# The second expert unit of a routed feed-forward tail takes the first expert's next 128 tokens, and the split weights of the first unit serve it too

## The chip, the cores and the metric

One Trainium2 chip, one NeuronCore. The metric is device time in microseconds (us) of one execution; lower is better. The core has a matrix engine (TensorE, PE), three engines for elementwise work (VectorE DVE, ScalarE ACT, GpSimd POOL), a queue that issues most transfers (SyncE, SP), and 16 DMA engines. An engine runs its instructions in program order.

## The reference

Three layers in a row on 2 x 768 tokens of width 512, all in float32:

```
x = attention(q, k, v)            # 8 heads of 64, window of 128 keys and 4 sink keys
x = moe_attention(x)              # 4 experts, each a causal attention over its own q, k, v; top 2 of 4
for b, s:                         # routed feed-forward ("moe2"), 8 experts
    fresh_e = argmax(x[b, s] @ w_gate)
    e = fresh_e if s == 0 or local_gate[b, s] < 0.5 else prev_e     # else the expert of the token before
    h = max(x[b, s] @ w1[e], 0)                                     # 512 -> 1024
    out[b, s] = softmax(logits)[e] * (h @ w2[e])                    # 1024 -> 512
```

Each token of the last layer goes through one expert only, and which one is known only on the chip.

## The kernel before

**Staging.** Tokens come in 12 tiles of 128 (`T = 12`, six of each batch). The two attentions run tile by tile. As tiles are finished their rows of x go to DRAM (`x2d`) and their router logits to `LG`, and `route` works out the expert of each token (`OH`), its rank in its expert (`rk`) and the rank modulo 128 (`slot`). `LT[j]` is a matrix for tile j that turns a list of chosen tokens into row numbers by a product on PE.

**Units.** The feed-forward then runs in units of 128 tokens of one expert: gather the rows by an indirect transfer on POOL (`ga`, L1563), transpose them (`ux`, L1543), a first group of 24 products with w1 (`unit_first`), ReLU (`hs`, L1603), transpose (`hT`), and a second group of 24 products with w2 (`unit_second`), then scale and scatter (`unit_end`, L1638 and L1641). Products are three float32r products each (L315 to L317), since every operand is split into a high and a low part. Remainders of up to 32 tokens go as at most four "pieces" in one unit of mixed experts (`pieces`, L1741), whose weights come through the ring `qw`.

**Weights of a unit.** Eight loads of 512 KB (`ld`, into the eight buffers `raw`), each skipped on the chip by a condition if the unit has the expert of the unit before (L1492); then eight splits (`sp`): ACT writes the high part (L1507), DVE the low part (L1515), into one of 11 buffers of the ring `w`. Five of these are buffers of the attention that have become free; six come with the pool `ff` and the buffer `wo`, after the attention's pools are closed (L1667 to L1679). A buffer goes back when the products that read it have been issued.

**Unit 0.** `first_expert` takes the expert with the most tokens among the first 8 tiles and lists its first 128 tokens, long before the last tile is routed, so that the first products of unit 0 lie under the rest of the attention. Its last quarter of weights, (3,1), shares memory with the router's scratch rows and loads after the last routing (`ld`, dependence on `K["routed"]`).

**The lists of all other units.** After the last tile, DVE works through two chains of small operations (L1400 to L1424), PE inverts the result (`inv`, L1430), DVE writes the row lists `gix` and `six` (L1432 to L1437), then the list of the pieces (L1445), then the table of experts `euf` (L1451 to L1459), which POOL copies to `eui` (L1569). SP reads `eui` for the addresses of every later load.

**The order of the work.** `Order.run` is a planner: each piece of work has an engine, an estimated duration, dependences, buffers and a priority. At each step it emits, for one engine, the piece that can start first by its estimates, and among those the one with the lowest priority number; so the program order of every engine is fixed before the launch. It runs twice over: once over everything up to unit 0's first half (L1666), where unit 0's work is marked to fill gaps only, and once over units 1 to 11 (L1808); whatever belongs to the second run stands behind the whole first run in each engine's queue. While PE has nothing to do before unit 1, the planner puts dummy products into the gap (`spin`, L396). Unit 0's second half (`unit_second(0, (1,))`) and its split (3,1) belong to the second run, and the split's low part waits for the gather of unit 1 (L1516).

## Time and profile before

| | |
|---|---|
| median of 3 runs | 427.0 us (423.95 to 429.46) |
| profiled execution | 427.42 us, span of the core 425.6 us, mean granted clock 0.987 |
| PE / DVE / ACT / POOL busy | 403.8 / 336.2 / 326.6 / 173.6 us |
| moved by DMA | 59.03 MB |

The span runs from the first to the last instruction on the core; the profiled execution is 1.8 us longer than its span. A busy PE includes dummy products.

### The profile page before, as it was taken

To read this page: it belongs to the slowest core of one execution; us is meant where nothing else is said; L and a number is where in the kernel's file an instruction comes from. 1 tells how busy PE (TensorE), PEld (TensorE's weight loads), DVE (VectorE), ACT (ScalarE), POOL (GpSimd) and SP (SyncE) were. 2 spreads that over 40 slices of the span, in tenths; PEclk is the share of its full clock that TensorE was granted. 3 is DMA by queue.
4 is the path that set the end of the run, shared out by engine and by line. 5 is a ranking of instruction groups with operands and counts; after the bars stand their busy time and mean duration, and the time that the engine had idled before them with its cause. 6 is when DMAs were issued, how large, how long until landed. Compare 5 with 4: busy or idle time off the path is not lost.

```text
span 425.6 us, 10370 instructions
## 1 busy us (share of the span) xinstructions
PE 403.8 (95%) x3322; PEld 316.1 (74%) x3322; DVE 336.2 (79%) x959; ACT 326.6 (77%) x767; POOL 173.6 (41%) x270
## 2 busy tenths in 40 slices
PE   7899999999999997999999999999999699999994
PEld 3579979978779867979767677556566488888883
DVE  3999598697898789588799879476886779898690
ACT  5799799679999697765796438477695978989780
POOL 8289995198886358401642043111020401100101
PEclk9999999999999999999999999999999979999999
DMA  9997288645978445220910247786658971100011
GB/s 181 170 203 197 67 154 159 122 101 101 180 111 160 101 89 111 52 75 13 339 74 27 74 153 267 245 244 203 202 168 261 393 296 46 49 27 26 24 28 55
DMA packets 102046, 59.03 MB, mean 139 GB/s; under 512 B 84319, under 2 KB 85855, under 8 KB 101984
## 3 DMA queue, kind: packets, MB, share of 16 engines
q1 hardware_dynamic: 99824, 51.47, 48.7%
q0 software_dynamic: 2160, 6.82, 4.6%
q8 instruction: 28, 0.46, 0.5%
q14 instruction: 34, 0.28, 0.2%
HBM read 86.58 MB, written 6.55 MB: 219 GB/s over the span
## 4 chain that ended last, share of the span: by engine, by line
PE 49%; issue 24%; DVE 18%; POOL 4%; ACT 3%; SPq 1%; POOLq 0%; another core or an unknown queue 0%; DMA 0%; ACTq 0%; DVEq 0%
PE bank L315 8%; PE bank L317 8%; PE bank L316 8%; PE bank L685 6%; DVE P L699 4%; PE bank L809 3%; PE bank L1741 3%; PE bank L410 3%; DVE pT L816 2%; DVE PX L699 2%; POOL out_dram L1641 2%; PE bank L1140 1%; PE bank L1543 1%; PE bank L780 1%; PE bank L826 1%
## 5 line engine op out<-in xcount | busy, mean ns | idle before, releaser
L1515 DVE TENSOR_TENSOR w<-raw,w 128x1024 fp32r<-128x1024 f32 x44 | 52.9, 1221 | 13.8 <-ACT w L1507 13.6
L709 ACT ACTIVATE P<-P,nm 128x260 f32<-128x260 f32 (+3 forms) x100 | 53.1, 535 | 10.9 <-DVE nm L699 10.6
L1507 ACT ACTIVATE w<-raw 128x1024 fp32r<-128x1024 f32 x44 | 45.8, 1062 | 9.6 <-DMA raw<-in_moe_w_dram 8.3
L769 POOL TENSOR_TENSOR raw<-PX,raw 128x512 f16<-128x512 f32 (+2 forms) x34 | 35.5, 1050 | 15.8 <-ACT raw L764 13.9
L1641 POOL DMA_INDIRECT out_dram<-yof,six x12 | 13.0, 1085 | 67.4 <-ACT yof L1638 66.2
L816 DVE TENSOR_TENSOR pT<-bank,pT 128x512 f16<-128x512 f32 (+1 forms) x50 | 30.7, 631 | 9.4 <-ACT pT L812 9.3
L1563 POOL DMA_INDIRECT xgf<-x2d,gix x9 | 10.4, 1152 | 66.3 <-PE bank L1543 60.8
L685 PE MATMUL bank<-kT,qT 64*128 64x260 f32 (+1 forms) x192 | 31.5, 398 | 2.1 <-POOL kT L583 1.1
L709 ACT ACTIVATE PX<-PX,nm 128x260 f32<-128x260 f32 (+4 forms) x60 | 30.5, 510 | 1.4 <-DVE nm L699 1.3
L315 PE MATMUL bank<-xT,wqk_h 128*128 128x256 f32 x96 | 29.5, 307 | 0.0
L410 PE MATMUL bank<-ident,raw 128*128 128x128 f32 x168 | 28.0, 289 | 0.5 <-DVE raw L949 0.3
L812 ACT ACTIVATE pT<-bank 128x512 f16<-128x512 f32 (+1 forms) x50 | 26.1, 550 | 2.8 <-PE bank L809 2.5
L809 PE MATMUL bank<-ident,P 128*128 128x128 f32 x180 | 26.8, 277 | 1.0 <-ACT P L709 0.7
L317 PE MATMUL bank<-xT,wqk_l 128*128 128x256 f32 x96 | 27.8, 289 | 0.0
L316 PE MATMUL bank<-xT,wqk_h 128*128 128x256 f32 x96 | 27.7, 288 | 0.0
L699 DVE CUSTOM_DVE_ANT_0 P<-bank,mask 128x260 f32<-128x260 f32 (+1 forms) x60 | 22.3, 399 | 5.4 <-POOL mask L332 4.7
L685 PEld LDWEIGHTS bank<-kT,qT 64*128 64x128 f32 x192 | 19.2, 185 | 9.2 <-issue 2.3
L1603 ACT ACTIVATE hs<-bank 128x512 f32<-128x512 f32 x24 | 14.3, 596 | 15.3 <-PE bank L317 15.3
L646 POOL TENSOR_SCALAR raw<-raw,s_sv 128x256 f32<-128x256 f32 x20 | 18.4, 930 | 18.0 <-ACT qT L416 9.1
L410 PEld LDWEIGHTS bank<-ident,raw 128*128 128x128 f32 x168 | 20.1, 162 | 7.0 <-DVE nm L699 2.0
L685 PE MATMUL bank<-k,q 64*128 64x256 f32 (+3 forms) x128 | 24.4, 466 | 0.1
L1515 DVE TENSOR_TENSOR xT<-raw,xT 128x1024 fp32r<-128x1024 f32 x16 | 19.2, 1217 | 6.6 <-ACT xT L1507 6.4
(456 smaller groups left out, 1476.8 us busy)
## 6 DMA issues: line engine op xcount, KB each, us to landing
raw<-in_moe_w_dram SPq DMA_DIRECT2D x104, 512.0 KB
qw<-in_moe_w_dram SPq DMA_DIRECT2D x64, 256.0 KB
raw<-in_v_dram SPq DMA_DIRECT2D x12, 256.0 KB
x2d<-x SPq DMA_DIRECT2D x12, 256.0 KB
raw<-in_q_dram SPq DMA_DIRECT2D x11, 256.0 KB
raw<-in_k_dram SPq DMA_DIRECT2D x11, 256.0 KB
pT<-raw SPq DMA_TRANSPOSE x46
raw<-in_moe_wv_dram SPq DMA_DIRECT2D x1, 512.0 KB
```

The lines of the kernel that those rows point to most:

```text
L315: nc.tensor.matmul(o, l[0], r[0], start=start, stop=False)
L316: nc.tensor.matmul(o, l[0], r[1], start=False, stop=False)
L317: nc.tensor.matmul(o, l[1], r[0], start=False, stop=stop)
L410: nc.tensor.transpose(p[:, j * 128:(j + 1) * 128], src(j), ident)
L685: nc.tensor.matmul(o, l, r, start=True, stop=True)
L699: nc.vector.tensor_tensor_reduce(p, s, sg["mask"], 0.0 if dead and st == 1 else -scale, gr["nm"] if si else 3.0e38, op0=OP.add, op1=OP.min ...
L709: nc.scalar.activation(p, p, AF.Exp, bias=gr["nm"], scale=-1.0, accum_out=sg["sum"]())
L769: nc.gpsimd.tensor_sub(shaped(pl[:, s_], dims), p_, shaped(ph[:, s_], dims))
L809: nc.tensor.transpose(R[tk][:, j * 128:(j + 1) * 128], R[gr["P"]][:, c:c + 128], ident)
L816: nc.vector.tensor_sub(pl[:, :n * 128], R[tk][:, :n * 128], ph[:, :n * 128])
L1507: nc.scalar.activation(R["w", u, c, hf][0], R["raw", u, c, hf], AF.Copy)
L1515: eng.tensor_sub(wl[:, :, s_], R["raw", u, c, hf][:, :, s_], f32(wh)[:, :, s_])
```

## The change

The first expert is given at least two units. Unit 1 is always the expert's tokens of rank 128 to 255. Their list needs only `rk`, `slot` and the first expert (`second_list`), so it is made directly behind the last tile's ranks, and the long chains that list all other units move, unchanged but for one operation, into a new function `lists`, in the planner's second run. `chosen` prepares one operation for each tile as it is routed. Unit 1 has no loads and no splits of its own: it reads unit 0's eight buffers of `w`, which unit 0 no longer gives back. Unit 2's loads compare with the expert of unit 0. Unit 0's second group of products and its split (3,1) go into the first run, without the wait for the gather. Buffers of the first attention move to a pool that is closed early (`fa`), and three of the ring's 11 buffers `w` now come from there, free before the attention ends; the ring keeps 11. The diff, cut:

```
-NW = 5
+NW = 2
+NWO = 3
...
     for t in range(n):
+        K["slot", j0 + t] = d_              # (in route; K["OH", j] likewise)
...
+            (0.08, lambda: V.tensor_scalar(fl0, oh0, float(C + PSZ + 1), None, op0=OP.mult))), [K["gix0"]], prio + 5)
+
+    def chosen(j, prio):
+        return add("DVE", 0.15, lambda: V.tensor_tensor_reduce(t80, OH[:, j, :], oh0, 1.0, 0.0, op0=OP.mult, op1=OP.add,
+                                                               accum_out=sl1[:, j:j + 1]), deps=[K["OH", j], K["first"]], prio=prio)
+
+    def second_list(prio):
+        cs = [chosen(j, at2(j // NT, j % NT, E1) + RPO + 3 if j < T - 1 else prio) for j in range(T)]
+        a = add("DVE", 0.1, lambda: V.scalar_tensor_tensor(u1f, rk, -float(C), slot, op0=OP.add, op1=OP.is_equal),
+                deps=[K["slot", j] for j in range(T)], prio=prio)
+        a = add("DVE", 0.1, lambda: V.tensor_tensor(u1_, u1f, sl1, op=OP.mult), deps=cs + [a], prio=prio)
+        def inv1():
+            for j in range(T):
+                nc.tensor.matmul(R["r_in1"][:, :1], LT[:, j, :], u1_[:, j:j + 1], start=j == 0, stop=j == T - 1)
+        c_ = add("PE", 0.4, inv1, deps=[a] + [K["LT", j] for j in range(T)], acq=[("B", "r_in1")], prio=prio)
+        K["gix1"] = add("DVE", 0.08, lambda: V.tensor_scalar(gix1, R["r_in1"][:, :1], -1.0, 0.0, op0=OP.add, op1=OP.max), ...
...
-    a = chain("DVE", ( ... L1400 to L1412 ... )), [K["cum", T], K["first"]], END)
-    ... L1414 to L1459 ...
+    second_list(END)
...
-                nc.sync.dma_start(raw, src, cond=R["e", u] != R["e", u - 1])
+                nc.sync.dma_start(raw, src, cond=R["e", u] != R["e", u - 1 if u > 2 else 0])
...
-        after = [K["ga", 1]] if u == 0 and (c, hf) == (3, 1) else []
+        after = []
...
+                              ("w", NWO, [([128, 2, 512], FR)] * 2)):      # in turnover
...
-        g0 = K["ga", u] = fo.add("POOL", 1.4, ga, deps=[K["gix"]] + ... + [K.get("eui")] * (u > 1) if u else ...
+        g0 = K["ga", u] = fo.add("POOL", 1.4, ga, deps=[K["gix"], K["eui"]] + ... if u > 1 else [K["gix1"]] + [K["out", j] for j in range(T)] if u else ...
-        for c in range(4 if u else 0):
+        for c in range(4 if u > 1 else 0):
             for hf in range(2):
                 ld(u, c, hf)
-        for c in range(2 if u else 0):
+        for c in range(2 if u > 1 else 0):
             for hf in range(2):
                 sp(u, c, hf)
...
-                        wh, wl = R["w", u, n, d // 2]
+                        wh, wl = R["w", 0 if u == 1 else u, n, d // 2]
-                rel = [("w", u, n, hf)] if (d0 + step) % 2 == 0 else []
+                rel = [("w", 0 if u == 1 else u, n, hf)] if u and (d0 + step) % 2 == 0 else []
...
-            for hf in range(2 if u or c == 2 else 1):
+            for hf in range(2 if u != 1 else 0):
                 sp(u, c, hf, bp + 5 * c + hf + BSP if u else bp + 5 * c + hf - 48)
...
-    unit_second(0, (0,))
+    unit_second(0)
...
+    def lists():
+        LP = -45
+        a = chain("DVE", (
+            (0.08, lambda: V.tensor_tensor(c8, cum[:, T, :], fl0, op=OP.max)),
+            ... L1400 to L1459 as before, the second chain behind K["gix1"] ...
+        K["eui"] = add("POOL", 0.1, lambda: P.tensor_copy(eui[:32 + PC], euf[:32 + PC]), deps=[K["euf"]], prio=LP)
+
     for u in range(TS):
         if u == 0:
             continue
+        if u == 1:
+            lists()
         unit_front(u)
         if u == 1:
-            sp(0, 3, 1, 10)
-            unit_second(0, (1,))
             probabilities()
```

## Rows read from the trace of the kernel before

**Rows 1.** The page, first line: the span of the core.
```profile
span 425.6 us, 10370 instructions
```

**Rows 2.** Windows: start:end, length, then busy time by engine, granted clock, DMA share, GB/s.
```profile
240.20:247.60 7.40, 6.97 (x53) 3.35 (x52) 6.47 (x39) 2.14 (x3) 1.84 (x4) 1.00 0.08 30
253.80:272.30 18.50, 17.89 (x114) 11.78 (x112) 16.74 (x29) 13.48 (x18) 4.47 (x4) 1.00 0.78 263
326.90:338.40 11.50, 8.49 (x43) 6.31 (x39) 7.59 (x8) 9.10 (x13) 2.90 (x3) 1.00 0.99 354
338.40:345.50 7.10, 6.43 (x16) 4.80 (x17) 5.82 (x6) 4.89 (x6) 1.57 (x1) 0.55 1.05 392
```

**Rows 3.** Windows of one line alone: L396 on PE, then L1515 on DVE.
```profile
240.20:247.60 7.40, 6.16 (x27) 2.40 (x27) 1.00 0.08 30
...
253.80:272.30 18.50, 11.81 (x10) 1.00 0.78 263
```

**Rows 4.** Timeline of PE, 240 to 254: start, length, line, out<-in, count.
```profile
240.20 0.82 PE L396 MATMUL bank<-v2h 128*128 128x512 f16 x3
241.05 0.66 PE L1543 MATMUL bank<-ident,hs 128*128 128x128 f32 x4
...
244.56 0.45 PE L1430 MATMUL bank<-v2h,v2h 128*128 128x23 f16 x12
...
247.59 0.58 PE L315 MATMUL bank<-xT,hT 128*128 128x512 f32 x1
...
253.79 0.40 PE L315 MATMUL bank<-w,uxf 128*128 128x512 f32 x1
```

**Rows 5.** Timeline of DVE, 235 to 249.
```profile
235.10 0.17 DVE L1273 CUSTOM_DVE_ANT_0 r_sc<-r_sc,r_fr 128x8 f32<-128x8 f32 x1
235.19 0.08 DVE L1273 DVE_READ_ACCUMULATOR2_ANT r_ms<- 128x1 f32 x1
...
239.09 0.36 DVE L1400 TENSOR_TENSOR v2h<-cum,k 128x192 f32<-128x192 f32 x1
...
239.75 0.14 DVE L1319 TENSOR_SCALAR slot<-rk 128x1 int32<-128x1 int32 x1
...
246.35 0.13 DVE L1459 TENSOR_SCALAR euf<-inc 1x1 f32<-1x1 f32 x1
...
247.01 1.28 DVE L1550 TENSOR_TENSOR hT<-bank,hT 128x512 fp32r<-128x512 f32 x2
248.21 1.22 DVE L1515 TENSOR_TENSOR wo_l<-raw,wo_h 128x1024 fp32r<-128x1024 f32 x1
```

**Rows 6.** Timeline of ACT, 241 to 249.
```profile
241.74 0.60 ACT L1546 ACTIVATE hT<-bank 128x512 fp32r<-128x512 f32 x1 [0.75 <-PE bank L1543]
242.23 1.05 ACT L1507 ACTIVATE wo_h<-raw 128x1024 fp32r<-128x1024 f32 x1
248.56 1.06 ACT L1507 ACTIVATE w<-raw 128x1024 fp32r<-128x1024 f32 x1 [5.28 <-DMA raw<-in_moe_w_dram]
```

**Rows 7.** Timelines of POOL and SP; last, issue to landing of the gathers into xgf.
```profile
246.07 1.05 POOL L1563 DMA_INDIRECT xgf<-x2d,gix  x1 [5.39 <-DVE dl L1456]
247.13 0.20 POOL L1569 CAST eui<-euf 36x3 int32<-36x3 f32 x1
...
248.38 0.10 SPq L1492 DMA_DIRECT2D raw<-in_moe_w_dram  x1
251.69 0.33 SPq L1729 DMA_DIRECT2D qw<-in_moe_w_dram  x1
...
321.33 23.01 SPq L1492 DMA_DIRECT2D raw<-in_moe_w_dram  x18
...
DMA to landing us min/median/max: 3.3/3.8/6.9
```

**Rows 8.** Timeline of PE and ACT at the first change of expert.
```profile
326.60 1.06 ACT L1507 ACTIVATE wo_h<-raw 128x1024 fp32r<-128x1024 f32 x1 [3.28 <-DMA raw<-in_moe_w_dram]
...
338.35 0.50 PE L315 MATMUL bank<-wo_h,ux 128*128 128x512 f32 x1 [1.83 <-ACT ux L1546]
```

More of the change, by code (lines that the diff above doesn't have):

```diff
@@ L292, in fused_kernel @@
     if banded and ns:
-        vbd = ring(work, 1, "vbd", ([96, H, D], F16))[0]
-        bufs["skp"] = ring(work, 2, "skp", ([128, 3, 32], F32))
+        vbd = ring(fa, 1, "vbd", ([96, H, D], F16))[0]
+        bufs["skp"] = ring(fa, 2, "skp", ([128, 3, 32], F32))
         for t in bufs["skp"]:
             nc.gpsimd.memset(t, 0.0)
-        bufs["skT"] = ring(work, 2, "skT", ([96, 128], F16))
+        bufs["skT"] = ring(fa, 2, "skT", ([96, 128], F16))
     R = {}
@@ L377, in fused_kernel @@
     wo_l = fw.tile([128, 2, XC], FR)
-    kT = work.tile([128, HP, (NT - 1) * BS + C], F32)
+    kT = fa.tile([128, HP, (NT - 1) * BS + C], F32)
     k2 = [work.tile([128, 2, S], F32, name=f"k2_{b}") for b in range(B)]
@@ L1215, in fused_kernel @@
     n0_ = rt.tile([128, 1], F32)
+    fl0 = rt.tile([128, E2], F32)
+    c8 = rt.tile([128, E2], F32)
+    sl1 = rt.tile([128, T], F32)
+    u1f = rt.tile([128, T], F32)
+    u1_ = rt.tile([128, T], F16)
+    gix1 = rt.tile([128, 1], I32)
     evv = rt.tile([128, E2], F32)
@@ L1299, in route @@
                  deps=[b_], rel=[rb], prio=prio)
+        for t in range(n):
+            K["OH", j0 + t] = b_
         def count():
@@ L1320, in route @@
                                            op0=OP.bitwise_and))), [t_ if n > 1 else c_, K.get(("cum", j0))], prio, rel=())
+        for t in range(n):
+            K["slot", j0 + t] = d_
         join([d_, t_], [cb], prio)
```

149 lines of the change are left out of this document (76 added, 73 removed).

## The prediction

> **What bounds the kernel now.** I read the span first [rows 1], then the timelines of all engines around the last tile's routing, then windows over the stretches after it. The sum is made against the profiled execution's 427.42 us (span 425.6, 1.8 outside it); it lies 0.4 above the median of the three runs, whose own spread is 5.5 us. About 2% is what a measurement of this kernel can tell from no change.
>
> PE sets the pace nearly everywhere from the last tile on, with two holes. The first is the one the change aims at. At 240.20 PE has finished unit 0's first products and goes to dummy products: 27 of them fill 6.16 of the next 7.40 us [rows 3]; real work there is one set of transposes and the inversion [rows 4]. Unit 0's second group starts at 247.59 and unit 1's first product at 253.79 [rows 4]. What PE waits for is DVE: from 239.09 to 246.48 it works through the list chains, and the low part of unit 0's transposed activations comes only behind them, at 247.01, the low part of split (3,1) at 248.21 [rows 5]. The high part had been ready since about 242.3 [rows 6].
>
> From 253.8 to 272.3 PE is busy 17.89 of 18.50 us [rows 2], with ten splits on DVE beneath it [rows 3]. So unit 1's splits are hidden work, and taking them out pays nothing directly. The second hole is at the first change of expert: from 326.9 to 338.4 PE works 8.49 of 11.5 us, with DMA busy 0.99 at 354 GB/s, then 16 products take 6.43 us at a granted clock of 0.55 [rows 2]. ACT stands there behind loads (3.28 us once) and unit 6's first product starts at 338.35 [rows 8].
>
> **The change part by part.**
>
> *Unit 1's list.* `slot` of the last tile is written at 239.75 [rows 5], done by 239.9. Behind it come two small DVE operations at 0.15 each with a hop, the inversion on PE (12 products, at most the 0.45 of the old one [rows 4]) and one DVE operation. With hops I put `gix1` at 241.4 and the gather at 241.5 instead of 246.07 [rows 7]. Landing 3.8 us later [rows 7] it is in at 245.3; the 6.9 of the slowest gather would make it 248.4, 1.2 later than I need it.
>
> *Unit 0's second group.* It follows the first group on PE directly. 24 products and unit 1's four transposes took 6.20 us (247.59 to 253.79) [rows 4]. With the transposes of `hs` (0.66 at most) and the inversion (0.45 at most), PE has 7.2 us of work, from 240.2 to about 247.4. Two inputs can be late. The first `hT` needs a low part on DVE (0.64 for one of the two [rows 5]): DVE is free of the long chains, so I allow 0.6 of waiting, between 0 and 1.5. Split (3,1) has its high part from 242.23 to 243.3 [rows 6] and would have its low part, 1.22 us [rows 5], at 244.6; it is wanted for the last six products, after 246, so it costs nothing. If its load came 2 us late it would cost 0.5.
>
> *Unit 1's start.* Its transposes belong to the second run and stand on PE behind all of unit 0. After them PE must wait for ACT (0.60 [rows 6]) and, after two products, for DVE (0.64); with hops that exposes 1.2 us, between 0.8 and 1.6. Unit 1's products then start in effect at 240.2 + 7.2 + 0.6 + 1.2 = 249.2 instead of 253.79: 4.6 earlier.
>
> *What comes back.* The lists' own inversion and the four-way `spread` that follows stay on PE, later: 0.6 in all. The PE waits of 0.61 in 253.8 to 272.3 [rows 2] came with the splits of unit 1 and go away. These cancel.
>
> *The twelve `chosen` operations.* Each is an operation with its read, 0.17 + 0.08 [rows 5]. Eight become ready together right after the first expert is known and four at one per tile; the whole is 3 us of DVE, which is not idle in that stretch. If all of it were on the path it would cost 3.0, if none, 0. Most tiles leave DVE gaps between dependent operations and the splits of unit 0 can move, so I take 0.3.
>
> *The moved chains.* They start behind split (3,1) on DVE, 244.6, and take the 7.4 us of before [rows 5] plus one evicted low part: end 252.7, `eui` on POOL at 252.9 (it was 247.33 [rows 7]). Queued behind it are SP's loads and unit 2's splits: ACT's first split came 1.2 us after `eui` [rows 6, 7], so now at 254.1, its low part done at 256.4. Unit 2's products are wanted one unit after 249.2, that is 24 + 24 products and three sets of transposes, 2 x 6.20 [rows 4]: at 261.6. The margin is 5.2 us, so this costs nothing as forecast. For the eight splits together: they are wanted by about 272, and the same 18.5 us of DVE held ten splits before [rows 3]; eight fit in 15. The ring is no limit: three buffers are free at once, unit 1 gives back the others as it goes.
>
> *Loads skipped.* Unit 1's loads took 0.10 us of SP each [rows 7] because they were skipped; unit 1 already had unit 0's expert. Dropping them saves no bytes, and the extra unit that the change could force on a smaller first expert does not arise.
>
> Sum: 4.6 gained, 0.3 lost, the rest cancels: 4.3 from 427.4, **423.1 us**. With the waits at their low ends (1.0 less), no cost of `chosen` (0.3) and the PE items, which I took at their full lengths, 0.8 shorter, it is 421; with the waits at their high ends (1.3 more) and 1.4 instead of 0.3 for `chosen` it is 425.5. All of `chosen` on the path would make it 427.1.
>
> **The rivals.**
>
> *The gain is lost again at the change of expert.* The first piece load was issued at 251.69, 4.4 after `eui` [rows 7]; now it would be 257.3, 5.6 later, while PE is 4.6 ahead. The loads of unit 6 stand behind all piece loads in SP's program order (first one at 321.33 [rows 7]), and DMA runs full from 326.9 [rows 2]. If the piece loads keep their pace, unit 6's loads start no earlier and its first product stays at 338.35: the time is then 427.4, or up to 428 with the 0.3 of `chosen`. Against it: before 272 DMA is busy only 0.78 [rows 2], and the piece loads are paced by PE's consumption as much as by the chip.
>
> *The second hole shrinks too.* PE loses there 3.0 + 0.7 us of waiting, and 16 products at 0.40 each instead of at most 0.24 lose 2.5 [rows 2, 4]: 6.2 us. ACT and DVE have eight splits less to do on the way and the planner lays out every queue anew; if unit 6's weights come early enough, the time falls to 417; with half of it, 420. Against it: the splits of units 2 to 5, and the 8 MB of two experts, stay.
>
> *Slower: unit 2 waits for its weights.* If the moved chains are stretched, because the planner puts evictions and split parts between their operations, `eui` slips. Up to 258.1 it costs nothing (margin 5.2). Beyond that each microsecond is one of PE, and after about 4.6 more, at 262.7, the gain is gone. Such a stall has a second price: after the waits of the second hole the granted clock was 0.55, that is the lower level, 1.2 GHz, for most of it, and 16 products lost 2.5 us [rows 2]. `eui` at 263 with one such spell gives 427.4 + 0.6 (0.3 of it `chosen`) + 2.5 = 430.5. The chains would have to take over twice their 7.4 us; DVE was 90% busy from 253.8 to 272.3 [rows 2], so it is not excluded.
> The Trainium skill, page "TensorE: Matmul & The Clock Gate", section "What's actually happening", says that throttled is the default state and activity releases it. By that rule an idle stretch where there used to be dummy products speaks against the change; the trace agrees at the second hole, and by the rule alone a spell there would cost the same 2.5 us that the row gives.
>
> **How the numbers follow.** Forecast, 421 to 425.5: 0.50. Gain lost at the change of expert, 425.5 to 428: 0.22. Second hole shrinks, 416 to 421: 0.18. Slower, 428 to 437: 0.10. The predicted time is the forecast's, 423.1. For the range I leave out the upper rival and the lower third of the third case: 417.5 to 428.0 leaves out about 0.16. Faster by over 2% means below 418.5: half to two thirds of the third case, and a little for a tail of the forecast, 0.14 together. Slower by over 2%, above 435.5: 0.03. Within 2%: 0.83.
>
> **What would show it.** Right: the gather of unit 1 near 241.5; no dummy products between unit 0's two groups beyond one or two microseconds; unit 0's last product near 247 and unit 1's first near 249; the list chains on DVE from about 244.6, `eui` near 253; 8 splits fewer on ACT and on DVE; unit 6's first product near 334 at the change of expert. Wrong: `slot` of the last tile later than 240.5 (`chosen` or the new buffer order on the path); a PE wait for a split in unit 2; unit 6's first product still near 338; a gap before unit 1 that is longer than 2 us.

## The result and the profile after

The changed kernel takes 432.33 us (median of 20 runs, 427.35 to 436.83); the kernel before takes 425.69 us beside it (median of 20, 422.20 to 429.46). The ratio is 1.012, 95% interval 1.0084 to 1.0156: slower by about 5 us (clear of the noise, though under 2%), where 423.1 was forecast and 428.0 was the top of the range. Eight of the twenty executions, the profiled one (435.82 us) among them, lie over 1.5% above the fastest at a granted clock of 0.973 to 0.983, and the ratio leaves such executions out. A second profile of the same kernel was taken later (430.81 us); both are used.

The first line of the page after answers to [rows 1]:
```profile
span 434.1 us, 10311 instructions
```
The timeline of DVE after, from the first expert's list to the last list (start, length, line, out<-in); it answers to [rows 5]:
```profile
203.08 0.16 DVE L1370 TENSOR_SCALAR gix<-bank 128x1 int32<-128x1 f32 x1 [1.17 <-PE bank L1368]
...
203.43 0.16 DVE L1378 CUSTOM_DVE_ANT_0 t<-OH,oh 128x8 f32<-128x8 bf16 x1
...
204.99 0.08 DVE L1378 DVE_READ_ACCUMULATOR2_ANT sl<- 128x1 f32 x1
...
247.82 0.15 DVE L1329 TENSOR_SCALAR slot<-rk 128x1 int32<-128x1 int32 x1
...
249.53 0.16 DVE L1391 TENSOR_SCALAR gix<-bank 128x1 int32<-128x1 f32 x1 [0.19 <-PE bank L1389]
...
253.67 0.16 DVE L1772 TENSOR_TENSOR c<-cum,fl 128x8 f32<-128x8 f32 x1
...
262.18 0.08 DVE L1829 TENSOR_SCALAR euf<-inc 1x1 f32<-1x1 f32 x1
```
The last tile's `slot` is written at 247.82, not at 239.75; 1.5 us of this lie before the first expert's list. The list chains take 8.6 us behind it (253.67 to 262.26), where they took 7.4. Eight `chosen` operations stand at 203.43 to 205.07.

The timeline of PE after, between the last `slot` and unit 2; it answers to [rows 4]:
```profile
245.82 0.39 PE L398 MATMUL bank<-v2h 128*128 128x512 f16 x1
...
250.15 0.39 PE L317 MATMUL bank<-xT,hT 128*128 128x512 f32 x1
...
253.37 0.60 PE L398 MATMUL bank<-v2h 128*128 128x512 f16 x2
...
256.55 0.60 PE L1519 MATMUL bank<-ident,xgf 128*128 128x128 f32 x4
256.99 1.67 PE L398 MATMUL bank<-v2h 128*128 128x512 f16 x7
258.31 0.58 PE L317 MATMUL bank<-wqk_h,uxf 128*128 128x512 f32 x1
...
272.19 2.80 PE L1714 MATMUL bank<-qw,v2h 128*32 128x512 f32 x10
276.08 2.89 PE L1714 MATMUL bank<-qw,v2h 128*32 128x512 f32 x6 [1.09 <-DMA qw<-in_moe_w_dram]
278.90 0.50 PE L317 MATMUL bank<-wo,hT 128*128 128x512 f32 x1
```
The 27 dummy products [rows 3] are down to ten (1, 2 and 7), and unit 0's second group (250.15) follows its first directly: this part of the change does what it says. From `slot` to unit 1's first product it is 10.49 us instead of 14.04. Then 16 piece products take from 272.19 to 278.90; with their weights there, 16 took 1.92 us in the trace before:
```profile
277.09 1.92 PE L1741 MATMUL bank<-qw,v2h 128*32 128x512 f32 x16
```

POOL, SP and ACT after, a view each; they answer to [rows 6, 7]:
```profile
250.46 1.05 POOL L1539 DMA_INDIRECT xgf<-x2d,gix  x1 [1.71 <-DVE gix L1391]
262.33 0.18 POOL L1830 CAST eui<-euf 36x3 int32<-36x3 f32 x1 [10.82 <-DVE euf L1829]
```
```profile
266.89 6.09 SPq L1702 DMA_DIRECT2D qw<-in_moe_w_dram  x11
274.02 5.25 SPq L1464 DMA_DIRECT2D raw<-in_moe_w_dram  x7
```
```profile
274.12 1.06 ACT L1479 ACTIVATE wo_h<-raw 128x1024 fp32r<-128x1024 f32 x1 [2.62 <-DMA raw<-in_moe_w_dram]
```
`eui` stands 4.2 us behind unit 1's first product (262.51 against 258.31); before it stood 6.5 ahead of it. SP sends eleven piece loads from 4.4 us after `eui`, and only then unit 2's loads, which are skipped but have to be reached; so ACT's first split of unit 2 starts 11.6 us after `eui`.

Windows of the profile after (length, busy time by engine, granted clock, DMA share, GB/s); they answer to [rows 2]:
```profile
240.20:247.80 7.60, 7.60 (x30) 5.71 (x31) 3.23 (x15) 1.37 (x3) 0.00 (x0) 0.69 0.11 37
247.80:258.30 10.50, 10.50 (x63) 7.75 (x62) 7.17 (x29) 3.34 (x5) 1.73 (x2) 1.00 0.24 74
258.30:276.80 18.50, 16.19 (x107) 9.81 (x106) 10.35 (x43) 6.80 (x11) 6.02 (x7) 1.00 0.62 205
334.00:346.00 12.00, 10.65 (x53) 6.38 (x51) 6.60 (x7) 6.96 (x10) 1.28 (x1) 1.00 1.02 381
```
In the 18.5 us behind unit 1's first product PE is busy 16.19, where it was 17.89 before. At the first change of expert the granted clock stays at 1.00 (0.55 before), with DMA as full as it was. From unit 6's first product to unit 7's, in the trace before, in after_again and in e2 (below: the kernel before with the `chosen` operations alone, whose plan behind unit 1 is close to that before):
```profile
338.35:354.65 16.30, 15.63 (x61) 12.36 (x62) 13.45 (x14) 12.96 (x16) 3.62 (x3) 0.79 0.68 252
345.62:358.00 12.38, 12.38 (x62) 10.20 (x60) 11.32 (x12) 11.19 (x15) 2.00 (x2) 1.00 0.66 242
346.27:358.74 12.47, 12.47 (x61) 10.20 (x60) 11.31 (x12) 11.15 (x15) 2.00 (x2) 1.00 0.61 227
```
So the profiled execution before has 3.8 us there that e2 does not have, and they go with a low clock: 0.21 of 16.3 us, 3.4, is clock that is missing.

**Where the time went.** The table cuts each profiled execution in four, from the timelines: from the first expert's list (`gix`, 203.08 above) to the last `slot`; from there to unit 1's first product; from there to unit 7's first activation; and to the end. Up to `gix` every kernel has the same instructions in the same order (200.5 to 203.6 us, which is how much executions differ). Beside the first and the third of these stands the mean granted clock of the stretch. `eui` is its end against unit 1's first product.

| kernel | list to last slot | its clock | slot to unit 1 | eui against unit 1 | unit 1 to unit 7 | its clock | to the end | span |
|---|---|---|---|---|---|---|---|---|
| before | 38.1 | 1.00 | 14.0 | -6.5 | 103.9 | 0.97 | 68.0 | 425.6 |
| after | 44.7 | 0.89 | 10.5 | +4.2 | 107.7 | 1.00 | 68.1 | 434.1 |
| after_again | 39.6 | 1.00 | 10.5 | +4.2 | 107.5 | 1.00 | 68.1 | 429.1 |
| e2_before_chosen | 42.7 | 0.96 | 14.6 | -7.4 | 100.8 | 1.00 | 68.2 | 430.0 |
| e1_chosen4 | 40.5 | 0.96 | 10.3 | +4.2 | 107.4 | 0.98 | 68.1 | 428.3 |
| e13_due_end | 39.3 | 1.00 | 10.5 | +4.2 | 108.3 | 0.98 | 68.1 | 426.6 |
| e9_chosen_end | 39.2 | 0.96 | 10.5 | +4.2 | 105.6 | 1.00 | 68.1 | 424.1 |
| e12_eui_late | 38.2 | 1.00 | 10.5 | +10.5 | 111.7 | 0.97 | 68.1 | 431.3 |
| e4_qu3 | 43.8 | 0.88 | 10.5 | +4.2 | 111.0 | 0.97 | 68.2 | 434.9 |
| e7_behind | 40.6 | 0.96 | 10.3 | +4.2 | 109.5 | 0.98 | 68.1 | 429.5 |
| e6_regs | 40.5 | 0.96 | 10.3 | +4.2 | 104.8 | 1.00 | 68.1 | 426.8 |
| e11_end_regs | 38.2 | 1.00 | 10.5 | +4.2 | 104.4 | 1.00 | 68.2 | 423.7 |
| e10_all | 38.1 | 1.00 | 10.5 | +4.2 | 116.6 | 0.96 | 68.0 | 435.5 |
| e15_prob_late | 38.1 | 1.00 | 10.5 | +3.7 | 106.9 | 1.00 | 68.1 | 425.2 |
| e3_lists_early | 43.2 | 0.92 | 16.8 | -9.4 | 101.8 | 1.00 | 68.2 | 431.9 |
| e16_lists_fill | 40.1 | 0.96 | 12.5 | -2.1 | 105.9 | 0.98 | 68.1 | 428.1 |
| e17_lists_fill2 | 39.5 | 0.96 | 12.5 | -2.1 | 101.4 | 1.00 | 68.1 | 422.5 |
| e18_spread_late | 40.4 | 0.96 | 10.7 | -0.3 | 103.5 | 1.00 | 68.2 | 425.4 |
| e19_inv_late | 39.4 | 0.96 | 10.9 | -1.0 | 104.3 | 0.98 | 67.7 | 424.1 |

From before to after the span grows by 8.5: 1.5 before the first changed instruction, 6.6 up to the last `slot`, 3.5 back up to unit 1, 3.9 lost from there to unit 7, and nothing behind. Two of these numbers are not the price of the change at a like clock. The 6.6 fell at a clock of 0.89; at 1.00, in after_again, it is 1.5. And the 3.9 is too small, for the stretch before has the low clock behind unit 6's first product in it: from unit 1's first product to unit 6's it is 84.6 us before and 85.4 in e2, but 92.3 and 92.0 in the two profiles after. So some 7 us are lost there. The expected gain of 3.5 is there, and the two losses outweigh it.

### The profile page after: what moved, and what is told of

The parts are those of the page before. It is cut to its first block, busy times and chain, and to the rows that moved or that the text cites. A ratio compares the mean times of both kernels' runs of the same rounds, so it can differ in the third digit from the quotient of the medians.

```text
span 434.1 us, 10311 instructions
## 1 busy us (share of the span) xinstructions
PE 409.8 (94%) x3317; PEld 319.3 (74%) x3317; DVE 332.0 (76%) x980; ACT 320.1 (74%) x759; POOL 171.2 (39%) x270
## 4 chain that ended last, share of the span: by engine, by line
PE 42%; issue 26%; DVE 13%; DMA 6%; ACT 6%; POOL 4%; SPq 2%; POOLq 0%; another core or an unknown queue 0%; ACTq 0%; DVEq 0%
PE bank L317 7%; PE bank L687 6%; PE bank L319 6%; PE bank L318 6%; PE bank L412 3%; DMA qw<-in_moe_w_dram 3%; PE bank L811 3%; DVE PX L701 2%; DVE pT L818 2%; DMA xg<-x2d,gix 2%; DVE P L701 2%; POOL out_dram L1614 2%; DMA pT<-raw 1%; PE bank L1714 1%; PE bank L782 1%
## 5 line engine op out<-in xcount | busy, mean ns | idle before, releaser
L771 POOL TENSOR_TENSOR raw<-PX,raw 128x512 f16<-128x512 f32 (+2 forms) x34 | 35.5, 1051 | 16.3 <-ACT raw L766 16.0
L1487 DVE TENSOR_TENSOR wo<-raw,wo 128x1024 fp32r<-128x1024 f32 x28 | 33.6, 1221 | 7.2 <-ACT wo L1479 7.2
L1614 POOL DMA_INDIRECT out_dram<-yof,six x12 | 12.5, 1046 | 62.8 <-ACT yof L1611 61.3
L1479 ACT ACTIVATE wo<-raw 128x1024 fp32r<-128x1024 f32 x28 | 28.8, 1057 | 3.5 <-DMA raw<-in_moe_w_dram 2.4
L412 PEld LDWEIGHTS bank<-ident,raw 128*128 128x128 f32 x168 | 20.7, 164 | 6.9 <-DVE nm L701 1.7
L1539 POOL DMA_INDIRECT xgf<-x2d,gix x9 | 8.9, 985 | 40.5 <-PE bank L1519 37.7
L811 PEld LDWEIGHTS bank<-ident,P 128*128 128x128 f32 x180 | 20.3, 142 | 3.2 <-ACT P L711 1.0
```

Source lines behind the costliest of these rows:

```text
L412: nc.tensor.transpose(p[:, j * 128:(j + 1) * 128], src(j), ident)
L771: nc.gpsimd.tensor_sub(shaped(pl[:, s_], dims), p_, shaped(ph[:, s_], dims))
L811: nc.tensor.transpose(R[tk][:, j * 128:(j + 1) * 128], R[gr["P"]][:, c:c + 128], ident)
L1479: nc.scalar.activation(R["w", u, c, hf][0], R["raw", u, c, hf], AF.Copy)
L1487: eng.tensor_sub(wl[:, :, s_], R["raw", u, c, hf][:, :, s_], f32(wh)[:, :, s_])
```

## The experiments

Theory A: the `chosen` operations bring the last `slot` late. Theory B: the late list (`eui`) costs the stretch from unit 1 to unit 7. A rival to A is that unit 0's work, now spread among the last tile's, does it; a rival to B that the stretch is bound by something that the list does not touch. Edits are cut to the lines that matter. Some expectations count the stretch to unit 7 from unit 1's first activation, about 3.6 us behind its first product: 102.0 there is the table's 105.6.

### e1: eight `chosen` taken out

The sums for tiles 0 to 7 exist already, for the first expert's own list.
```
-            (0.1, lambda: V.reduce_sum(sl0, se0, axis=AX.X)),
+            (0.1, lambda: V.reduce_sum(sl1[:, :JE], se0, axis=AX.X)),
-        cs = [chosen(j, ...) for j in range(T)]
+        cs = [chosen(j, ...) for j in range(JE, T)]
```


> Theory A (the eight `chosen` instructions for tiles 0 to 7, which stand on VectorE at 203.4 to 205.1 us of the changed kernel, make the planner order the work of tiles 8 to 11 anew, and that is what brings the last tile's `slot` 6.6 us later): here `chosen` is issued for tiles 8 to 11 alone and the sums of tiles 0 to 7 are taken from the sums that the first expert's list already needs, so the order on VectorE up to tile 9 is again that of the kernel before. Then the last tile's `slot` falls back from 247.8 to about 240 to 242 us, unit 1's first product from 258.3 to 251 to 253, TensorE's granted clock between 230 and 250 us stays at 1.00, and the time is 5 to 7 us below the changed kernel: ratio to the kernel before 0.995 to 1.003. What then remains against 423 us is the late list (theory B: 4 us lost in the first pieces). Rival (unit 0's second group or the other split that now fill gaps in the first run, or the new places of the buffers, delay the last tile): `slot` stays at 246 us or later and the ratio at 1.010 to 1.015.

Measured: 430.47 us, ratio 1.014 (1.0092 to 1.0188). Theory A's ratio (0.995 to 1.003) did not come. In the profile the last `slot` comes 40.5 us behind the list and the span is 5.8 below that of after, but the runs show no gain (1.014 beside 1.012): the first profile of after has the low clock in it. `slot` is 2.4 us later than before, still, and the loss behind unit 1 is all there (107.4).

### e2: `chosen` alone, added to the kernel before

```
+    for j in range(T - 1):
+        chosen(j, at2(j // NT, j % NT, E1) + RPO + 3)
```


> The kernel before with nothing but the `chosen` instructions added (tiles 0 to 10, same place and same due times as in the changed kernel; their result is not used). Theory A: their busy time is 2.3 us, but the order of tiles 8 to 11 becomes that of the changed kernel, so the last tile's `slot` comes at 245 to 248 us instead of 239.8, unit 1's first product 5 to 8 us later, and the ratio to the kernel before is 1.012 to 1.018. Rival (fills or buffers are the cause): `slot` at 239.5 to 242, ratio 0.999 to 1.004.

Measured: 431.46 us, ratio 1.0149 (1.0100 to 1.0198): the kernel before becomes slower by as much as the whole change makes it, from operations whose result nobody uses. DVE's `slot` operations in this kernel, tiles 8 and 9, 10, 11:
```profile
232.83 0.15 DVE L1323 TENSOR_SCALAR slot<-rk 128x2 int32<-128x2 int32 x1
235.78 0.14 DVE L1323 TENSOR_SCALAR slot<-rk 128x1 int32<-128x1 int32 x1
246.36 0.14 DVE L1323 TENSOR_SCALAR slot<-rk 128x1 int32<-128x1 int32 x1
```
Before, tiles 8 and 9, then 10 (tile 11 is in [rows 5]):
```profile
222.35 0.16 DVE L1319 TENSOR_SCALAR slot<-rk 128x2 int32<-128x2 int32 x1
231.02 0.15 DVE L1319 TENSOR_SCALAR slot<-rk 128x1 int32<-128x1 int32 x1
```
Tiles 8 and 9 are routed 8.5 us later behind the list than before (29.2 against 20.7), and ACT's split of unit 0 that waits for that routing starts at 228.7 instead of 217.1. That is Theory A; unit 0's moved work is not in this kernel, so it is not needed for the delay. The clock of this stretch is 0.96, so the 4.6 us by which the last `slot` is later hold a part that is the clock's.

### e13: all `chosen` kept, only their due time changed

```
-        cs = [chosen(j, at2(j // NT, j % NT, E1) + RPO + 3 if j < T - 1 else prio) for j in range(T)]
+        cs = [chosen(j, prio) for j in range(T)]
```


> The changed kernel with one thing altered: the due time of the `chosen` instructions of tiles 0 to 10 is that of the end and not that of their tiles. All 12 are still issued, eight of them still at 203 to 206 us, so their busy time (2.5 us) is all there; but the order of the other instructions on VectorE is again that of the kernel before up to its row 731 (tile 10's routing). If the new order is what delays the last tile (theory A as the second round left it), `slot` falls back as in the run with the three late instructions: 38 to 40 us behind the first expert's list (`gix0`; before 38.2, changed 44.7), ratio 1.005 to 1.011. If the busy time of the instructions does it, `slot` stays 42 us or more behind `gix0` and the ratio 1.011 to 1.016.

Measured: 429.02 us, ratio 1.0093 (1.0062 to 1.0124). DVE's `slot` operations:
```profile
222.34 0.17 DVE L1329 TENSOR_SCALAR slot<-rk 128x2 int32<-128x2 int32 x1
231.03 0.15 DVE L1329 TENSOR_SCALAR slot<-rk 128x1 int32<-128x1 int32 x1
239.75 0.15 DVE L1329 TENSOR_SCALAR slot<-rk 128x1 int32<-128x1 int32 x1
```
All twelve operations are issued, eight of them still between 200.8 and 207.1, and the last `slot` is back at 39.3 us behind the list, at a clock of 1.00. Of their busy time 1.2 us reaches the path (39.3 against 38.1 before, and against 38.1 and 38.2 in e10, e11, e12 and e15, which have this order without the eight). What the change has beyond that comes with their due time: given that of their tiles, the planner lets them go ahead, and lays out the work of tiles 8 to 11 behind them in another order. The second profile of the change, below, shows how that order costs time. In the runs the gain over the change (1.0141 there) is small, and the intervals overlap.

### e9: e1 with the other three due at the end

```
-    chosen(j, at2(j // NT, j % NT, E1) + RPO + 3 if j < T - 1 else prio)
+    chosen(j, prio)
```


> The first experiment's kernel, with the `chosen` instructions of tiles 8 to 10 given the due time of the end instead of that of their tiles; the order on VectorE is then that of the kernel before up to its row 731 (tile 10's routing). Theory A, carried on: of the 2.8 us by which the last tile's `slot` was still late in the first experiment (242.6 against 239.8 us) the three instructions between tiles 8 to 10 make 1 to 2.5, and `slot` comes at 239.8 to 241.5, unit 1's first product at 250.5 to 252, ratio 1.004 to 1.012 (the loss in the pieces stays). Rival (the rest is unit 0's earlier work among the last tile's, or one execution's difference from another): `slot` at 242 or later and the ratio as in the first experiment, 1.010 to 1.017.

Measured: 427.72 us, ratio 1.0079 (1.0042 to 1.0116), `slot` at 239.9 and unit 1's first product at 250.4, both as expected to 0.1 us. Beside after_again (1.0141), e13 and e9 take a third or a little more of the loss away. What stays is put down to Theory B, which e12 tests.

### after_again: a second profile of the change

> The changed kernel once more, unaltered, for a second profile beside the others on one chip. Theory A: `slot` 43 to 45 us behind `gix0`, theory B: 103 to 105 us from unit 1's to unit 7's first activation, and the two rounds of first pieces in 5.5 to 7 us; ratio 1.010 to 1.016. If the first profile was only a disturbed execution, `slot` stands 38 to 40 us behind `gix0` here.

Measured: 431.13 us, ratio 1.0141 (1.0084 to 1.0198). B's numbers repeat to 0.3 us (107.5 after 107.7), though e1, e9 and e13, which have the same order of instructions from unit 1 to unit 7, spread from 105.6 to 108.3. A's do not repeat: `slot` is 39.6 us behind the list here, 44.7 in the first profile, from one program. The expectation had named 38 to 40 as the sign that the first profile was a disturbed execution, and it was. Windows of after (list to last `slot`, then three within), then of after_again, then of e13 and of e2 (list to last `slot`):
```profile
203.08:247.82 44.74, 38.65 (x359) 29.98 (x359) 34.97 (x136) 28.98 (x68) 14.39 (x20) 0.89 0.32 113
230.00:234.70 4.70, 2.58 (x30) 2.10 (x29) 4.67 (x22) 4.70 (x14) 4.31 (x7) 1.00 0.15 56
230.00:240.00 10.00, 7.02 (x61) 5.80 (x61) 9.26 (x28) 7.05 (x16) 5.13 (x8) 0.73 0.08 28
240.00:250.00 10.00, 10.00 (x52) 7.56 (x51) 4.84 (x21) 1.97 (x4) 0.68 (x1) 0.75 0.24 79
```
```profile
203.46:243.10 39.64, 34.62 (x359) 26.72 (x358) 34.76 (x137) 28.93 (x68) 14.39 (x20) 1.00 0.36 127
230.00:235.10 5.10, 2.89 (x49) 2.39 (x47) 5.07 (x19) 5.10 (x11) 4.74 (x7) 1.00 0.14 51
230.00:240.00 10.00, 7.21 (x72) 5.91 (x71) 9.84 (x29) 6.46 (x13) 4.74 (x7) 1.00 0.08 28
```
```profile
200.47:239.75 39.28, 35.52 (x360) 26.22 (x360) 35.34 (x136) 28.52 (x68) 14.18 (x20) 1.00 0.38 129
```
```profile
203.64:246.36 42.72, 36.17 (x358) 28.37 (x358) 33.85 (x135) 29.01 (x68) 14.34 (x20) 0.96 0.34 118
```
PE waits 3.0 and 2.8 of the 10 us from 230, but in the first the granted clock falls behind it and in the second it does not. The clock that is missing in the first, 0.11 of 44.7 us or 4.9 us, is nearly all of the 5.1 us by which the two differ. Where the clock holds, the new order takes 39.6 against e13's 39.3 with the same twelve operations: of the 1.5 us that the change then loses, 1.2 are the busy time of `chosen` and 0.3 the order. The other executions with this order, or nearly this order, have 42.7 (e2), 43.2 (e3) and 43.8 (e4), at clocks of 0.96, 0.92 and 0.88. In the old order, or nearly the old order, the clock is 0.96 or more in all ten profiles (e9 to e13 and e15 to e19), with 38.1 to 40.4 us. The clock over whole executions, profiled or not, agrees: its mean is under 0.985 in 13 of 24 of the change and in 1 of 10 of e13. So the due time costs mainly by way of the clock, which is low more often with the new order. Why it falls there in one execution and not in the next stays open.

### e12: the list made later on purpose

```
-            P.tensor_copy(eui[:32 + PC], euf[:32 + PC])
+            for _ in range(24):
+                P.tensor_copy(eui[:32 + PC], euf[:32 + PC])
```


> The kernel with the late `chosen`, with `eui` made later on purpose: GpSimd copies it 24 times instead of once (about 4 us more, unknown to the planner, whose order stays the same). Theory B, as a dose: unit 1 and all before it stay where they are; the first pieces' loads and unit 2's loads go out about 4 us later; the stretch from unit 1's to unit 7's first activation grows by 3 to 4.5 us from 102.0; ratio 1.014 to 1.020 (1.008 without). Rival (the loss between unit 1 and unit 2 has another cause, and `eui` has slack): the stretch stays within 1.5 us of 102.0, ratio 1.006 to 1.012.

Measured: 432.87 us, ratio 1.0153 (1.0084 to 1.0223), against 1.0079 of e9. POOL, then PE:
```profile
255.58 6.44 POOL L1832 CAST eui<-euf 36x3 int32<-36x3 f32 x24 [10.88 <-DVE euf L1829]
```
```profile
272.04 1.75 PE L1714 MATMUL bank<-qw,v2h 128*32 128x512 f32 x8
274.65 3.61 PE L1714 MATMUL bank<-qw,v2h 128*32 128x512 f32 x8 [0.86 <-DMA qw<-in_moe_w_dram]
```
The copies took 6.44 us, not the 4 I had reckoned with, and in the profile the dose came out one to one: `eui` 6.3 us later against unit 1, the stretch 6.1 us longer than e9's (111.7 against 105.6), all of it between the first activations of units 1 and 2 (28.9 us against 22.5). In the runs the ratio rises by 0.0074, about 3 us, with wide intervals. Unit 1 and what precedes it stay in place. The copies also hold the gather of unit 2, which stands behind them on POOL, and PE waits for it:
```profile
265.50 1.12 PE L1519 MATMUL bank<-ident,xgf 128*128 128x128 f32 x4 [5.29 <-DMA xgf<-x2d,gix]
```
The granted clock falls behind this wait (0.50 from 264.6 to 271.4). But these two do not set the time: the 16 piece products end 16.2 us behind `eui` here, and 15.4 to 16.6 behind it in the five other executions with this order (after, after_again, e1, e9, e13). It is the loads that the list releases which end the stage, and the list has no slack in this order: Theory B.

### e4 and e7: the pieces moved behind other work

```
-QU = 2
+QU = 3
```


> The changed kernel with the pieces spread over units 3 and on instead of 2 and on (one constant). Theory B: the stall of TensorE at 272 to 279 us is gone, because no piece is due there and unit 2's skipped loads no longer stand behind eleven loads on SP: 3 to 5 us below the changed kernel, ratio 1.000 to 1.005, if the end can take the later pieces. Rival (the stall is that of unit 2's own weights, or the piece rounds just stall elsewhere, or they lengthen the end): no gain, ratio 1.008 to 1.016.

```
-            pr = at + 100 * (s_ // QN) + 16
+            pr = at + 100 * (s_ // QN) + 30
```


> The first experiment's kernel (eight `chosen` instructions taken out) with one constant changed: the rounds of pieces are ranked behind the second group of products of the unit before them (+30 in place of +16), so that TensorE runs unit 1's second group (12 products, 2.8 us) before the first two rounds and not behind them. In the first experiment's trace these two rounds of 16 products take 5.7 us from 266.65 us, where 16 piece products that find their weights take 1.9. Theory B (TensorE stands in front of loads that `eui` released too late, with ready work behind): the two rounds lose about 2.8 us less, and if unit 2's weights are there by then the time falls by 2 to 3.5 us to a ratio of 0.999 to 1.007. Rival (the loss is only moved: unit 2's own loads, which stand behind the eleven piece loads on SP, become the next wait, or the later rounds stall in the same way): ratio 1.010 to 1.016.

Measured: e4 434.37 us, ratio 1.0136 (1.0065 to 1.0207); e7, built on e1, 434.85 us, the median of four runs, too scattered (428.81 to 439.21) for a ratio. Both do what they were to do at their place: from unit 1's to unit 2's first activation it is 13.5 us in e4 and 19.0 in e7, against 22.9 in after. And both lose it, and more, later: unit 1 to unit 7 takes 111.0 and 109.5, at clocks of 0.97 and 0.98. From unit 6's first product to unit 7's it is 22.9 and 21.3 us there, 12.4 in after. The rivals were right: a stall taken from one round of pieces comes back in another.

### e6, e11 and e10: the planner told of the register reads

It reckons with no time between `eui` and the first piece load; the traces of the change show 4.4 and 3.7 us.
```
+        regs_ = fo.add("RG", 4.0, lambda: None, deps=[K["eui"]], prio=at - 100)
...
-            lds = [fo.add("DMA", 0.73, wl(s_, p_), deps=[K["eui"]], ...
+            lds = [fo.add("DMA", 0.73, wl(s_, p_), deps=[regs_], ...
```
e6 is e1 with this, e11 is e9 with this, e10 is e11 with e7's edit too.

> The first experiment's kernel, with the planner told that the pieces' loads go out 4.0 us behind `eui` (in the traces 3.8 to 4.4 us pass between `eui` and the first of these loads, while SP reads its registers; the planner reckons with none). Its order then runs unit 2's first group of products (24) ahead of the first pieces, and unit 2's skipped loads ahead of part of the pieces' loads. Theory B: the two first rounds of pieces wait no longer, 3 to 4 us are won back, ratio 1.000 to 1.006. Rival (unit 2's splits on ScalarE and VectorE or its weights bound this stretch, not the order of the pieces): TensorE waits in unit 2's first group instead, ratio 1.009 or more.

> Eight `chosen` instructions out, the other three due at the end, and the planner told of the 4.0 us of register reads ahead of the pieces' loads; the pieces keep their rank of the changed kernel. The parts add up if both theories hold: from the kernel with the late `chosen` the last `slot` 39.2 us behind `gix0` and unit 1's first activation 14.1 behind that, from the kernel with the told planner 101.3 us from unit 1's to unit 7's first activation and 68.1 to the end: with `gix0` at 201.6 that is a span of 424.3, against 425.6 of the kernel before: ratio 0.994 to 1.001. Rival (as in the kernel with all three edits, a stretch of pieces that costs 113 us and not 101 since the plan has moved against the loads): ratio 1.005 or more.

> The three edits together: eight `chosen` instructions out and the other three due at the end, the pieces ranked behind the second group of the unit before them, and the planner told of the 4.0 us of register reads. Both theories: last `slot` at 240 to 242, unit 1's first product at 250.5 to 252.5 (1 to 3 us ahead of the kernel before), no loss of over 1.5 us in the first pieces: 421 to 425 us, ratio 0.990 to 1.000. Rival (the pieces' loads bound the stretch from `eui` to the end of the pieces whatever the order, so a list that is 10 us later against unit 1 costs its time anyway): ratio 1.003 or more.

Measured: e6 426.39 us, ratio 1.0043 (1.0001 to 1.0085); e11 426.09 us, ratio 1.0026 (0.9992 to 1.0060); e10 435.85 us, ratio 1.0265 (1.0211 to 1.0319). Unit 2's first group now runs ahead of the first pieces and the stretch falls to 104.8 and 104.4. The two repairs bring the time to that of the kernel before, and not below it; e11 misses its range (0.994 to 1.001) by a little. In e10 the two edits of the order work against each other: 116.6 us, far from the gain that was expected.

### e3, e16, e17, e18, e19 and e15: the list early again

e3 is after with the lists in the first run, ranked at `END + 1`. e17 is e9 with them in the first run, ranked behind unit 0 and filling DVE's gaps; e16 is that with the planner told. In both `eui` is copied behind the gather of unit 1.
```
     unit_first(0)
     unit_second(0)
+    lists()
...
-        LP = -45
+        LP = END + 210
```
e18 is e17 with the products that spread the pieces' list moved back behind unit 1's transposes, e19 moves the lists' own inversion too. e15 is e11 with the probabilities held until `eui` is made.

> The changed kernel with the chain of lists issued in the first run, right behind the second unit's list, instead of in the second run between the probabilities; only the copy of the unit experts on GpSimd stays behind unit 1's gather. Theory B (the late `eui` brings the pieces' loads late, they stand ahead of unit 2's skipped loads on SP, and TensorE loses 4 to 5 us in the two rounds of pieces at 272 to 279 us): `eui` comes 4 to 6 us earlier against unit 1's first product, the two rounds of pieces take 2 to 3 us instead of 6.7, and the time is 3 to 5 us below the changed kernel: ratio 1.000 to 1.005. Rival: the chain now stands on VectorE ahead of unit 1's low part and holds it, so unit 1's first product slips by 1 to 4 us and the ratio stays at 1.008 to 1.015 or rises.

> The kernel of the second repair (eight `chosen` out, three due at the end, planner told of the register reads), with the chain of lists put back into the first run, ranked behind unit 0's work there, so that it fills VectorE while the gather of unit 1 is under way; the copy `eui` stands behind that gather on GpSimd. Theory B: `eui` comes 4 to 5 us earlier (at 8 to 9 us behind the last `slot`, not 14.7, so 1 to 2 us ahead of unit 1's first product instead of 4.2 behind it), unit 1's first product stays within 1 us of 10.5 us behind `slot`, and the stretch from there to unit 7's first activation falls from 104.4 to 100 to 103 us: ratio 0.990 to 0.998. Rival (VectorE's lists now hold unit 1's low part, or the loads of unit 2 and the pieces bound the stretch from elsewhere): unit 1's first product over 1 us later or the stretch at 104 us or more, ratio 1.000 or more.

> The same without telling the planner of the register reads: the first four pieces then stand ahead of unit 2's first group on TensorE again. Theory B: as `eui` is 4 to 5 us earlier, even this order waits little: stretch 101 to 105 us against 105.6 to 108.3 with the late list and this planner, ratio 0.993 to 1.003. Rival: as long as with the late list, 105 us or more, ratio 1.004 or more.

> The kernel with the list in the gather's shadow and the unaltered planner, with one step taken back out of the way: the spreading of the pieces' list over the partitions (8 small products on TensorE and 3 instructions on VectorE) goes to the second run, behind unit 1's transposes. In the trace without this TensorE waited for these products ahead of unit 1's transposes and unit 1's first product came 12.5 us behind the last `slot` instead of 10.5. If that wait is the price of the early list: first product at 10.5 to 11.3 us, `eui` and the stretch to unit 7 as there (101.4 us, up to 103), ratio 0.991 to 0.998. Rival (VectorE's list instructions, which still stand ahead of unit 1's low part, set it): first product at 12 us or more, ratio as there, 0.995 to 1.002.

> The same with the unit lists' 12 products and the 4 instructions behind them in the second run too, so that only the chain to `eui` itself fills VectorE ahead of unit 1. If TensorE's waits for list products are the price: first product of unit 1 at 10.3 to 11 us behind the last `slot`; the order of the pieces is another one here (unit 2's first group ahead of them), so the stretch may be 100 to 105 us: ratio 0.990 to 1.003. Rival as above: first product at 12 us or more.

> The second repair's kernel with the probabilities held back on VectorE until `eui` is made, so that they no longer stand between the instructions of the lists: `eui` comes about 1.5 us earlier against unit 1's first product (2.7 behind it, not 4.2). Theory B: the stretch falls by 1 to 1.5 us from 104.4, ratio 0.997 to 1.001. Rival (the scales of units 0 and 1, which need the probabilities, come too late and hold the banks of unit 2): ratio 1.002 or more.

Measured: e3 432.47 us, ratio 1.0165 (1.0112 to 1.0218); e16 426.85, 1.0047 (1.0010 to 1.0083); e17 424.17, 0.9982 (0.9951 to 1.0014); e18 425.76, 1.0048 (1.0012 to 1.0084); e19 423.97, 0.9991 (0.9961 to 1.0020); e15 426.23, 1.0041 (1.0007 to 1.0075). POOL and SP of e17:
```profile
243.16 1.05 POOL L1539 DMA_INDIRECT xgf<-x2d,gix  x1 [1.70 <-DVE inc L1646]
250.73 0.18 POOL L1544 CAST eui<-euf 36x3 int32<-36x3 f32 x1 [6.52 <-DVE qv L1680]
```
```profile
255.33 6.00 SPq L1769 DMA_DIRECT2D qw<-in_moe_w_dram  x11
262.70 7.36 SPq L1464 DMA_DIRECT2D raw<-in_moe_w_dram  x9
```
`slot` is at 240.55 there, so `eui` ends 10.4 us behind it instead of 14.7, and the stretch takes 101.4 us instead of 105.6 (e9, same planner): four microseconds earlier, four shorter. Unit 1 pays for it, with 12.5 us instead of 10.5. e16 has the same list and the same start of unit 1, but the told planner, and takes 105.9: with the early list, telling the planner makes it slower (1.0047 against 0.9982), so the order of the pieces counts as well as the list. In e18 the two microseconds of unit 1 come back:
```profile
251.81 0.46 PE L1680 MATMUL bank<-v2h,v2h 128*128 128x23 f16 x12
252.12 0.64 PE L1519 MATMUL bank<-ident,xgf 128*128 128x128 f32 x4
...
253.30 0.24 PE L1431 MATMUL bank<-qv,ident 32*32 32x1 f32 x8
```
The transposes (252.12) no longer wait for the spread (253.30), and unit 1 starts 10.7 us behind `slot`. But the stretch grows by the same two, to 103.5: from `slot` to unit 7 it is 113.9 us in e17 and 114.2 in e18. Unit 1's start is thus not what sets unit 7's, and e18's ratio lies above what was expected for it. In e3, whose lists are ranked ahead of unit 0's work, unit 1 comes 16.8 us behind `slot`: the trap that the change avoids. e15 moved `eui` by 0.5 us only, and its stretch is 2.5 us longer than e11's.

e17 and e19 are the best that I found: as fast as the kernel before, not faster. With the early list the stretch from unit 1's first product to unit 6's is back at 84.3 to 87.7 us in e16 to e19 (92.0 and 92.3 in the change). In its profile e19 even reaches unit 6 134.6 us behind the first expert's list, 2.2 ahead of the kernel before, and loses this from unit 6 to unit 7, which take 16.9 us where the change takes 12.4, with some low clock in it: there the change of expert is the next bound.

## Why the prediction was wrong

**The first hole closes: right, 1.1 short.** Forecast were a gather 1.75 us behind `slot`, unit 1's first product 9.45 behind it and a gain of 4.6; measured 2.64, 10.49 and 3.5. The missing microsecond is in small pieces: unit 0's second group starts 2.3 behind `slot`, takes 6.4 up to unit 1's transposes, and from these to the first product it is 1.8. The gather, 0.9 late, is not in the way, as PE comes from unit 0's products to the transposes without a wait (256.55).

**`chosen` at 0.3, between 0 and 3.0: the first failed step.** Measured are 1.5 us up to the last `slot` where the clock holds and 6.6 where it falls to 0.89; 39.6 to 44.7 us in five executions with this order or nearly this, against 38.1. I bounded the term by the busy time of the twelve, and for that part the bound was good: e13 has all of it and loses 1.2. What I left out is that an operation with an early due time moves the others, and that the moved order brings the low clock into a stretch for which I had reckoned with none: e2 has no other part of the change and loses 4.6 at a clock of 0.96. The sign I had named for it, a `slot` later than 240.5, is the one that came.

**`eui` has a margin of 5.2 and costs nothing: the second failed step, and the larger one.** `eui` itself was forecast well: 3.7 us behind unit 1's first product (252.9 against 249.2), measured 4.2. The price was wrong: about 7 us up to unit 6's first product (92.3 and 92.0, against 84.6 before and 85.4 in e2). I took ACT's first split of unit 2 at 1.2 us after `eui`, as unit 1's was before [rows 6, 7]; but before, unit 1's skipped loads went out ahead of the piece loads, and now eleven piece loads stand ahead of unit 2's: 11.6 us. And PE meets the first piece products ahead of ready work: 6.7 us for 16 products that take 1.92 with their weights there. Later rounds wait for their loads too (1.35 us once, ahead of the round at 338.97 in after); the rest of the 7 us was not followed round by round. e12 shows no margin at all.

**The rivals.** That the gain is lost again by later piece loads (0.22) has the right mechanism but too small a size. It put unit 6's first product at 338.35 still and the time at that of the kernel before; measured are 350.62 and 345.62 (1.5 and 1.8 of it a later start), and e9, without most of the loss by `chosen`, is still 1.0079 to the kernel before. Its place was too late: the loss begins between units 1 and 2. The second hole did not shrink by the change. From unit 5's first activation to unit 7's it is 34.9 us before and 32.6 and 32.8 in the two profiles after, but what went is the low clock behind unit 6's first product (16.3 against 12.4), which e2, with the plan of before, does not have either; from unit 5's first product to unit 6's it is 19.2 before, 20.3 and 20.5 after. The sum was made against that one execution, and the 2.5 us which it found lost to the low clock there are, by these traces, that execution's and not the kernel's. The slower case asked for `eui` beyond 258.1 in a plan where unit 1 starts at 249.2; it needed no such slip, and the low clock came ahead of unit 1 and not in unit 2.

**The bound of both kernels.** From the last `slot` to unit 7's first activation it is 117.9 us before and 118.2 and 117.9 after: the 3.5 us won at unit 1 are spent by then. At a like clock they are more than spent: e2, whose clock holds there, takes 115.4. It is 113.9 to 115.1 in e6 and e11 (told planner) and in e17, e18 and e19 (early list), but 117.4 in e15 and 118.3 in e16, which are near to them in list and planner, and 122.2 in e12 with the latest list. So what a start of unit 1 is worth depends on the list, on the loads behind it and on the order of the pieces, and I read it from unit 1 alone. What remains open is whether any order of pieces and units keeps all of the 3.5 us; none of those tried did.

## What to carry to other kernels

Where a planner lays out the instructions, price an added operation by what it displaces: give it the latest due time that its use allows, and compare the order of the other instructions before its busy time. When a chain is split to start one consumer early, follow the other consumer to the first wait that ends the stage; here the list for the later units lost 10.7 us against unit 1, and that ate the 3.5 gained. Before two profiles are compared, put the granted clock beside each stretch: here a low clock in the profile before hid half of one loss, and one in the first profile after made four fifths of the other. A wait in a stream of loads that is moved elsewhere in the order is not a wait removed; time the whole stream.

## What the runs showed of the hardware

One program, the change, gave 44.7 and 39.6 us for the same stretch; in the first the granted clock over 230 to 250 us was 0.73 and 0.75, that is the lower of the two levels, 1.2 GHz, for about half of that time, after PE had been busy 2.58 of 4.70 us from 230. The Trainium skill, page "TensorE: Matmul & The Clock Gate", section "What's actually happening", says that the throttled state is the default and that activity releases it. The fall behind a stretch of waits is in line with that; the second profile, with 2.89 of 5.10 us busy from 230, kept 1.00, so such a wait does not bring it each time.

Between `eui` and the first piece load 4.4 us pass in after and in e17 (262.51 to 266.89, 250.91 to 255.33), and 3.2 to 3.7 in after_again, e1, e9 and e12. The program has SP read five values into registers there; the traces do not show the reads themselves. Twenty-four copies of 36x3 on GpSimd took 6.44 us, 0.27 each, where a single one shows 0.18.
